# Row maxima of attention: transposed by VectorE and laid out through DRAM, with p x v groups cut at the ends of query blocks

## The chip, the cores and the metric

The kernel runs on one core of a Trainium2 chip. A core has five engines with queues of their own: TensorE (PE in the profile; PEld are its weight loads), VectorE (DVE), ScalarE (ACT), GpSimd (POOL) and SyncE (SP), which here only issues DMAs. The metric is device time in microseconds (us) of one execution.

## The reference

Two layers, each attention and then an MLP with Mish, both with a residual and a layer norm, over 2048 rows of 512 in float32. 32 heads of width 16:

```
scores = einsum("bhqd,bhkd->bhqk", q, k) * Dh ** -0.5
p = softmax(scores, axis=-1)
o = einsum("bhqk,bhkd->bhqd", p, v)
```

`x = x + A(norm(x)); x = x + B(norm(x))`, twice with the same weights. The softmax needs, for each query and head, the maximum of its row of scores before the first exp of that row.

## The kernel before

**Blocks and steps.** In attention the heads are taken in 8 groups of 4 (`NG`, `HG`), the queries in 4 blocks of 512 columns (`NCH`, `CW`). A block (one group, 512 queries; 32 per layer) has 16 steps, one per tile of 128 keys, with 4 heads in each; 512 steps per layer.

**The scores are computed twice.** First for the maxima (*M*, `max_mm`, L273): queries as stationary operand, 128 queries by 512 keys, two heads side by side in two halves of TensorE's rows (L293); VectorE reduces the 128x1024 scores from PSUM to two columns of maxima (L297). The PSUM tiles of M (`pm`) have two buffers. 32 M's make a block. Then for the exp (*P* and *S*): keys as stationary operand, 512 queries as columns, so that p stands with keys on the partitions as p x v needs it. *P* (`pair`, L338) computes two heads (L347) into two banks, of which there is one set (tag `s2`), and ScalarE takes the exp of both (L348). *S* (`single`, L350) does a third head (L357, L358) in one bank (tag `s1`).

**How the maximum gets into the exp.** The matmuls of P and S have 48 rows of split q and k, and two more, rows 48 and 49 of each half: ones on k's side (L249) and, on q's side, minus the maximum of each query in two parts, rounded and remainder. So the score comes out of TensorE with its maximum subtracted. For this the maxima, which lie with queries on the partitions (128x16: 4 heads by 4 tiles of 128 queries), must come to lie along a row. When the last M of a block has been reduced, `max_fold` (L306) reduces the four partial maxima (L308, 128x64 to 128x16). Four ticks later (a tick comes with every v, L422) `max_rows` (L311) transposes them on TensorE into the bank `s1` (L316), ScalarE copies them negated (L319), GpSimd makes the two parts (L320, L321) on 16x128, and SP issues eight DMAs of 2 KB from there into q's rows (L325).

**p x v** (*v*, `pv`, L360) accumulates over the keys of a block in one PSUM bank (`acc`): 4 heads in four column quarters, `va` with 32 columns per head as the stationary operand. Its work is counted in units of a quarter (128 query columns, all four heads); a step has 4 units and a block 64. Each v calls `pv(3 * done)`, so it does what is missing up to three units per v so far. At the end of a block it stops (`full`) until the bank has been drained: ScalarE copies it (L392), SP stores it (L393). The drain is called behind the next P, the following v takes up what was left.

**The order** is written out by hand, three steps at a time:

```
CYCLE = ("PMvSM", "PvMSPMv", "SMPvMS")
```

That is 4 P, 4 S, 6 M and 4 v per cycle of three steps, 12 units of p x v. `pe` chains TensorE's instructions in just this order; the other engines' queues are ordered by the framework's scheduler, except those calls that `behind` keeps in program order. M runs ahead by 24 steps (`AHEAD`), so a block's maxima are complete eight steps before its first P. SP's queue also carries the loads of q and k of the next group (`prep_qk`, two rows of ones among them), of v, and of weights; GpSimd's carries the splitting of weights (L132, L133) in the first layer.

Of the kernel before, what the change touches and what calls it, by code (L numbers as in the profile page):

```python
# [9 lines left out]
F32 = mybir.dt.float32  # L10
F32R = mybir.dt.float32r
BF16 = mybir.dt.bfloat16
AF = mybir.ActivationFunctionType
ALU = mybir.AluOpType
AX = mybir.AxisListType
# [3 lines left out]
P = 128  # L19
S, D, H, DH, F = 2048, 512, 32, 16, 1792  # L20
NCH = 4
CW = S // NCH
# [3 lines left out]
HG = 4  # L26
# [6 lines left out]
KROWS = 48  # L33
MROWS = 50
HALF = 64
K_PARTS = (0, 0, 1)
Q_PARTS = (0, 1, 0)
CYCLE = ("PMvSM", "PvMSPMv", "SMPvMS")
QW = CW // 4
AHEAD = 24  # L40
PRE = 4
FILL = 12
# [5 lines left out]
MAX_M = (6, 3, 7)  # L48
T_BUFS = {"he": 1, "hr": 1}
NBLK = 22  # L50


@with_exitstack
def kernel(ctx: ExitStack, tc: tile.TileContext, x, wqkv, wo, w1, b1, w2, out):
    nc = tc.nc
# [3 lines left out]
    const = ctx.enter_context(tc.tile_pool(name="const", bufs=1))  # L59
    blk = ctx.enter_context(tc.tile_pool(name="blk", bufs=NBLK))  # L60
    tmp = ctx.enter_context(tc.tile_pool(name="tmp", bufs=2))
    ps = ctx.enter_context(tc.tile_pool(name="ps", bufs=2, space=PSUM))
    dram = ctx.enter_context(tc.tile_pool(name="dram", bufs=1, space=DRAM))

    nc.scalar.preload_act_table_set("natural_log_exp_and_others")
    ident = const.tile([P, P], F32, name="ident")
# [2 lines left out]
    nc.gpsimd.memset(mhalf, -0.5)  # L69
    lnhalf = const.tile([P, 1], F32, name="lnhalf")  # L70
    nc.gpsimd.memset(lnhalf, LN_HALF)
    ones = const.tile([MROWS - KROWS, P], F32, name="ones")
    nc.gpsimd.memset(ones, 1.0)
    b1t = const.tile([P, FT], F32, name="b1t")
    nc.sync.dma_start(b1t, b1.rearrange("(f p) -> p f", p=P))

    def b8(shape, dt, name):
        return blk.tile(shape, dt, tag="blk", name=name)
# [3 lines left out]
    def open_banks():  # L82
        banks["pool"] = tc.tile_pool(name="sp", bufs=1, space=PSUM, reuse_waits="tile")
        banks["s"] = banks["pool"].__enter__()

    def close_banks():
        banks.pop("pool").__exit__(None, None, None)
        del banks["s"]
# [3 lines left out]
    def pbank(tag, name):  # L92
        if tag == "s":
            return banks["s"].tile([P, 512], F32, tag=tag, name=name, bufs=3)
        return ps.tile([P, 512], F32, tag=tag, name=name, bufs=1)
# [4 lines left out]
    def behind(ins):  # L100
        return tc.keep_in_program_order(ins)
# [110 lines left out]
    class Attention:  # L212
        def __init__(self, l, scr):
            self.l, self.scr = l, scr
            self.vscr = dram.tile([NG, P, NKT, HG * VW], F32, name=f"vscr{l}")
            self.oscr = [dram.tile([KT, 2, P, CW], F32, name=f"oscr{l}{c}") for c in range(NCH)]
            self.va = {}
            self.qk, self.mxs, self.pts, self.accs = {}, {}, [], {}
            self.singles, self.full, self.unit = 0, None, 0
            self.later = []  # L220
            self.chained, self.running, self.last = False, False, None

        def tick(self, n=1):
            due, self.later = [f for t, f in self.later if t <= n], [(t - n, f) for t, f in self.later if t > n]
            for f in due:
                f()

        def pe(self, ins):
            if self.chained:
# [9 lines left out]
        def prep_qk(self, g):  # L239
            l = self.l  # L240
            ks, qs = [], []
            for u in range(HG // 2):
                k = b8([P, S], F32R, f"ks{l}{g}{u}")
                q = b8([P, S], F32R, f"qs{l}{g}{u}")
                m, h0 = divmod(g * HG + 2 * u, P // DH)
                for e in range(2):
                    r0 = e * HALF
                    queue = nc.gpsimd if g == 0 and e else nc.sync
                    queue.dma_start(  # L249
                        k[r0 + KROWS : r0 + MROWS].bitcast(F32).rearrange("p (r n) -> p r n", n=P),  # L250
                        ones[:, None, :].to_broadcast([MROWS - KROWS, S // P, P]),
                    )
                    yield
                    for t, parts, base in ((k, K_PARTS, NCH), (q, Q_PARTS, 0)):
                        for j, a in enumerate(parts):
                            queue.dma_start(
                                t[r0 + j * DH : r0 + (j + 1) * DH].bitcast(F32),
                                self.scr[base + m][a, (h0 + e) * DH : (h0 + e + 1) * DH, :].bitcast(F32),
                            )
                            yield  # L260
                ks.append(k)
                qs.append(q)
            self.qk[g] = (ks, qs)
# [34 lines left out]
            if u == 1 and i == GSTEPS // 4 - 1:  # L298
                self.max_fold(b)

        def bank(self, name):
            if self.running:
                return self.pool.tile([P, CW], F32, tag="s1", name=name)
            return pbank("s", name)

        def max_fold(self, b):  # L306
            nm = tmp.tile([P, HG * NCH], F32, tag="nm", name=f"nm{self.l}{b}")
            nc.vector.tensor_reduce(nm, self.mxs.pop(b).rearrange("p h t a -> p (h t) a"), axis=AX.X, op=ALU.max)  # L308
            self.later.append((4, lambda: self.max_rows(b, nm)))

        def max_rows(self, b, nm):  # L311
            g, qb = divmod(b, NCH)
            l = self.l
            _, qs = self.qk[g]
            tp = self.bank(f"nmt{l}{b}")
            self.pe(nc.tensor.transpose(tp[0 : HG * NCH, 0:P], nm, ident))  # L316
            nf = tmp.tile([HG * NCH, P], F32, tag="nf", name=f"nf{l}{b}", bufs=1)
            np_ = tmp.tile([HG * NCH, 2, P], F32R, tag="np", name=f"np{l}{b}", bufs=1)
            nc.scalar.activation(nf, tp[0 : HG * NCH, 0:P], AF.Copy, scale=-1.0)  # L319
            behind(nc.gpsimd.tensor_copy(np_[:, 0], nf))  # L320
            behind(nc.gpsimd.tensor_tensor(np_[:, 1], nf, np_[:, 0].bitcast(F32), op=ALU.subtract))  # L321
            for h in range(HG):
                for a in range(2):
                    r = (h % 2) * HALF + KROWS + a
                    nc.sync.dma_start(  # L325
                        qs[h // 2][r : r + 1, ts(qb, CW)].bitcast(F32).rearrange("o (t n) -> o t n", n=P),
                        np_[h * NCH : (h + 1) * NCH, a, :].bitcast(F32),
                    )

        def head_rows(self, i):  # L330
            s, h = divmod(i, HG)
# [28 lines left out]
        def pv(self, upto):  # L360
            while self.unit < min(upto, 4 * STEPS):
# [3 lines left out]
                if kt == 0 and q0 == 0:  # L365
                    if self.full is not None:
                        return
                    self.accs[b] = pbank("acc", f"pv{self.l}{b}")
                cols = slice(q0 * QW, q1 * QW)
                for h in range(HG):  # L370
# [23 lines left out]

        def run(self, hooks, pre, fill):
            self.prep_v(0, range(NCH - 1))
            self.running = True
            left = 2 * PRE
            close_banks()
            with tc.tile_pool(name="sa", bufs=1, space=PSUM, reuse_waits="tile") as self.pool:  # L400
                half, done = 2 * (AHEAD + PRE), -4
                for s in range(STEPS + 4):
                    if s % GSTEPS == GSTEPS - NKT and s // GSTEPS + 1 < NG:
                        self.prep_v(s // GSTEPS + 1)
                    for item in CYCLE[s % 3]:
                        if item == "P":
                            self.pair()
                            self.drain()
                        elif item == "S":
                            self.single()  # L410
                        elif item == "M" and left:
                            left -= 1
                            next(pre)
                            next(pre)
                            if not left:
                                next(pre, None)
                                self.prep_v(0, [NCH - 1])
                        elif item == "M":
                            self.max_mm(half // 2, half % 2)
                            half += 1  # L420
                        else:
                            self.tick()  # L422
                            done += 1
                            self.pv(3 * done)
                    if s + FILL >= STEPS:
                        next(fill, None)
                    for fn in hooks.get(s, []):
                        fn()
                self.drain()
                self.tick(99)  # L430
            open_banks()

    def load_qkv(l, wts, which, later):
# [12 lines left out]
    def qkv(l, wts, tt, order, late, due):  # L446
        scr = [dram.tile([2, P, S], F32R, name=f"scr{l}{m}") for m in range(2 * NCH)]
        att = Attention(l, scr)
        ahead = [0]

        def some_max():
            if ahead[0] < AHEAD + PRE:
                att.tick()
                for n in range(2):
                    att.max_mm(ahead[0], n)
                ahead[0] += 1

        done = 0
# [33 lines left out]
        i = 0  # L492
# [185 lines left out]
    for l in range(2):  # L678
        due = {}
# [9 lines left out]
        att = qkv(l, wts, tt, order, late, due)  # L689
# [30 lines left out]
        for c, (t0, t1, t2, t3) in enumerate(((-42, -20, -19, -13), (-26, -19, -18, -11), (-10, -6, -4, 0))):  # L720
            o = outs[c]
# [89 lines left out]
```

## Time and profile before

| | |
|---|---|
| median of 3 runs | 3623.95 us (3623.9 to 3626.84) |
| the profiled execution | 3625.2 us; span of its instructions 3623.4 us |
| granted TensorE clock, mean | 0.997 of full speed |
| first P of the two layers | 186.2 and 1987.6 us |
| last drain of the two layers | 1460.1 and 3262.0 us |
| shares of the span | PE 98%, PEld 54%, DVE 82%, ACT 70%, POOL 16% |
| transposes of maxima (L316) | 64, 277 ns each |

Attention is thus some 1274 us of each layer; the rest is the projections, the MLP, and the norms. In a row of the groups' view stand line, engine, operation, output and inputs, shapes and count; then busy us, mean ns of one, and the engine's idle time before them with what ended it. In a row of the line of time stand start and length in us, both of equal instructions merged (x count), and in brackets the idle time before. The view of stretches gives length and busy us of each engine between two times.

### The profile page before, as it was taken

Reading aid. Unit: us, or ns where it says so; the run is one execution under the profiler, and the core shown is the slowest. Engines: PE = TensorE matmul, PEld = TensorE weight load, DVE = VectorE, ACT = ScalarE, POOL = GpSimd, SP = SyncE. Lnnn points to the kernel's source line nnn. Section 1 sums busy time; section 2 is a strip of 40 time slices with the busy share of each in tenths; the row PEclk is TensorE's granted clock in tenths of the full one; section 3 lists DMA queues with packets and bytes.
Section 4 is the critical chain, followed back from the end, with each engine's and each line's share of the span. In section 5 each row is a group of like instructions: output and inputs, shape, how many; then the busy total and the mean of one; then the engine's idle time right before and its main releaser. Section 6 shows DMA issues by size and latency. Waiting matters only on the chain. (4 is left out here: it accounts for less than half of the span.)

```text
span 3623.4 us, 69472 instructions
## 1 busy us (share of the span) xinstructions
PE 3553.0 (98%) x28784; PEld 1948.5 (54%) x28784; DVE 2963.7 (82%) x2978; ACT 2520.7 (70%) x3475; POOL 567.6 (16%) x589
## 2 busy tenths in 40 slices
PE   7999999999999999999999999999999999999999
PEld 5644444444444444777776444444444444447887
DVE  4779999999999994666647799999999999946565
ACT  2178888888888888344421788888888888873444
POOL 2200101001000002345421000000000000024455
PEclk9999999999999999999999999999999999999999
DMA  6551313313122224600164311112021211245000
GB/s 192 202 157 38 79 49 69 68 40 78 48 51 60 51 78 65 183 35 12 47 197 150 66 31 35 36 40 43 19 46 28 46 33 33 78 69 179 36 12 24
DMA packets 128707, 254.07 MB, mean 70 GB/s; under 512 B 18680, under 2 KB 62584, under 8 KB 114568
## 3 DMA queue, kind: packets, MB, share of 16 engines
q1 hardware_dynamic: 101896, 174.58, 19.8%
q0 software_dynamic: 8224, 35.21, 3.5%
q10 hardware_dynamic: 18272, 39.85, 3.0%
q8 instruction: 226, 3.70, 0.4%
q14 instruction: 89, 0.73, 0.1%
HBM read 148.38 MB, written 99.09 MB: 68 GB/s over the span
## 5 line engine op out<-in xcount | busy, mean ns | idle before, releaser
L297 DVE TENSOR_REDUCE mxv<-pm 128x2 f32<-128x1024 f32 x2048 | 2388.0, 1219 | 180.7 <-PE pm L293 132.7
L348 ACT ACTIVATE p<-sp 128x1024 f32<-128x1024 f32 x1366 | 1396.9, 1023 | 17.5 <-PE sp L347 12.3
L373 PE MATMUL pv<-p,va 128*32 128x128 f32 (+3 forms) x16048 | 1166.9, 392 | 0.0
L293 PE MATMUL pm<-ks,qs 48*128 48x512 f32 x4096 | 1106.8, 445 | 0.2
L358 ACT ACTIVATE p<-ss 128x512 f32<-128x512 f32 x1364 | 815.2, 598 | 384.7 <-PE ss L357 290.3
L347 PE MATMUL sp<-qs,ks 50*128 50x512 f32 x2732 | 737.8, 447 | 4.5 <-ACT p L348 2.2
L293 PEld LDWEIGHTS pm<-ks,qs 48*128 48x128 f32 x4096 | 460.0, 184 | 360.6 <-issue 256.8
L373 PEld LDWEIGHTS pv<-p,va 128*32 128x32 f32 x16048 | 368.2, 108 | 498.2 <-issue 417.8
L357 PE MATMUL ss<-qs,ks 50*128 50x512 f32 x1364 | 610.7, 448 | 0.1
L357 PEld LDWEIGHTS ss<-qs,ks 50*128 50x128 f32 x1364 | 252.0, 185 | 305.3 <-ACT p L358 210.6
L347 PEld LDWEIGHTS sp<-qs,ks 50*128 50x128 f32 x2732 | 276.7, 183 | 202.3 <-ACT p L348 117.3
L320 POOL CAST np<-nf 16x128 fp32r<-16x128 f32 x64 | 17.9, 280 | 2230.5 <-ACT nf L319 2188.2
L608 POOL TENSOR_TENSOR hb<-hb,he 128x512 f32<-128x512 f32 x112 | 157.6, 1407 | 188.2 <-DVE he L605 184.1
L611 POOL TENSOR_TENSOR hb<-hb,hr 128x512 f32<-128x512 f32 x112 | 160.4, 1432 | 137.3 <-DVE ah L610 129.5
L612 DVE TENSOR_TENSOR al<-hb,ah 128x512 fp32r<-128x512 f32 x112 | 108.0, 964 | 84.5 <-POOL hb L611 82.2
L606 ACT ACTIVATE hr<-he 128x512 f32<-128x512 f32 x112 | 70.8, 632 | 151.6 <-POOL hb L611 77.0
L154 ACT ACTIVATE pt<-qk 128x512 fp32r<-128x512 f32 x64 | 37.9, 598 | 158.9 <-PE qk L162 127.5
L604 ACT ACTIVATE he<-he 128x512 f32<-128x512 f32 x112 | 70.8, 632 | 102.9 <-DVE he L603 99.7
L602 ACT ACTIVATE hb<-h,b1t 128x512 f32<-128x512 f32 x112 | 76.8, 685 | 77.2 <-DVE al L612 52.0
L610 DVE TENSOR_TENSOR ah<-hb,hr 128x512 fp32r<-128x512 f32 x112 | 76.9, 687 | 61.4 <-ACT hr L607 34.3
L605 DVE SCALAR_TENSOR_TENSOR he<-he 128x512 f32<-128x512 f32 x112 | 79.9, 714 | 41.9 <-ACT he L604 39.1
L603 DVE TENSOR_SCALAR he<-hb 128x512 f32<-128x512 f32 x112 | 68.0, 608 | 48.5 <-POOL hb L608 33.9
(225 smaller groups left out, 3277.7 us busy)
## 6 DMA issues: line engine op xcount, KB each, us to landing
scr<-pt ACTq DMA_DIRECT2D x64, 512.0 KB
qs<-scr SPq DMA_DIRECT2D x180, 128.0 KB
ks<-scr SPq DMA_DIRECT2D x180, 128.0 KB
vscr<-v SPq DMA_DIRECT2D x32, 512.0 KB
va<-vscr SPq DMA_DIRECT2D x64, 256.0 KB
oscr<-ot SPq DMA_DIRECT2D x64, 256.0 KB
ww<-sw POOLq DMA_DIRECT2D x14, 1024.0 KB, 5.2
qs<-np SPq DMA_DIRECT2D x512, 2.0 KB
```

Source lines behind the costliest of these rows:

```text
L293: nc.tensor.matmul(pm[:, e], qs[u][rows, q0 : q0 + P], ks[u][rows, ts(n, 512)], start=True, stop=True)
L297: nc.vector.tensor_reduce(self.mxs[b][:, 2 * u : 2 * u + 2, qt, n], pm, axis=AX.X, op=ALU.max)
L347: self.pe(nc.tensor.matmul(sp[:, e], k, q, start=True, stop=True))
L348: nc.scalar.activation(self.pts[-1][:, 0:n], sp[:, 0:n], AF.Exp, scale=SCALE)
L357: self.pe(nc.tensor.matmul(sp, k, q, start=True, stop=True))
L358: nc.scalar.activation(self.pts[i // 3][:, 2], sp, AF.Exp, scale=SCALE)
L373: nc.tensor.matmul(self.accs[b][ts(h, VW), cols], self.va[b // NCH][:, kt, h, :], self.pts[j][:, e, cols], start=kt == 0 and q0 == 0, stop ...
L605: nc.vector.scalar_tensor_tensor(e, e, 2.0, e, op0=ALU.add, op1=ALU.mult)
L608: nc.gpsimd.tensor_tensor(hb, hb, e, op=ALU.mult)
L610: nc.vector.tensor_tensor(ah, hb, r, op=ALU.mult)
L611: nc.gpsimd.tensor_tensor(hb, hb, r, op=ALU.mult)
L612: nc.vector.tensor_tensor(al, hb, ah.bitcast(F32), op=ALU.subtract)
```

## The change

Two parts. **The maxima** no longer pass through TensorE, PSUM and ScalarE. The fold writes 16 of the 32 columns of a tile whose others are zero (two such tiles, in turn); VectorE transposes each 32x32 block of it (128x32), so that in every quarter of 32 partitions 16 rows hold the maxima of 32 queries. GpSimd makes the two parts from that, now on 128x32 and in two buffers. SP writes them to DRAM in four DMAs, one per quarter, and reads them back in four, one per head, each with both of q's rows. The sign moves from ScalarE's copy to k's rows, which become minus ones. `tick` and its delay go: all of it follows the fold at once. **The groups of p x v**: `pv(3 * done)` becomes `pv(units(done))`; over 64 v's, 192 units and three blocks, a v does three units except for the 21st and 42nd, which do four, and the 63rd and 64th, which do two. So the 21st, 42nd and 64th end a block.

```diff
+def units(done):
+    n, i = divmod(max(done, 0), 64)
+    if i < 22:
+        u = 3 * i + (i == 21)
+    elif i < 43:
+        u = 64 + 3 * (i - 21) + (i == 42)
+    else:
+        u = 128 + 3 * (i - 42) - (i == 63)
+    return 192 * n + u
...
-    ones = const.tile([MROWS - KROWS, P], F32, name="ones")
-    nc.gpsimd.memset(ones, 1.0)
+    minus = const.tile([MROWS - KROWS, P], F32, name="minus")
+    nc.gpsimd.memset(minus, -1.0)
+    folded = [const.tile([P, TR], F32, name=f"folded{i}") for i in range(2)]
+    for t in folded:
+        nc.gpsimd.memset(t, 0.0)
...
         def max_fold(self, b):
-            nm = tmp.tile([P, HG * NCH], F32, tag="nm", name=f"nm{self.l}{b}")
-            nc.vector.tensor_reduce(nm, self.mxs.pop(b).rearrange("p h t a -> p (h t) a"), axis=AX.X, op=ALU.max)
-            self.later.append((4, lambda: self.max_rows(b, nm)))
-
-        def max_rows(self, b, nm):
             g, qb = divmod(b, NCH)
             l = self.l
             _, qs = self.qk[g]
-            tp = self.bank(f"nmt{l}{b}")
-            self.pe(nc.tensor.transpose(tp[0 : HG * NCH, 0:P], nm, ident))
-            nf = tmp.tile([HG * NCH, P], F32, tag="nf", name=f"nf{l}{b}", bufs=1)
-            np_ = tmp.tile([HG * NCH, 2, P], F32R, tag="np", name=f"np{l}{b}", bufs=1)
-            nc.scalar.activation(nf, tp[0 : HG * NCH, 0:P], AF.Copy, scale=-1.0)
-            behind(nc.gpsimd.tensor_copy(np_[:, 0], nf))
-            behind(nc.gpsimd.tensor_tensor(np_[:, 1], nf, np_[:, 0].bitcast(F32), op=ALU.subtract))
+            nm = folded[b % 2]
+            nc.vector.tensor_reduce(
+                nm[:, 0 : HG * NCH], self.mxs.pop(b).rearrange("p h t a -> p (h t) a"), axis=AX.X, op=ALU.max
+            )
+            nt = tmp.tile([P, TR], F32, tag="nt", name=f"nt{l}{b}")
+            nc.vector.transpose(nt, nm)
+            np_ = tmp.tile([P, 2, TR], F32R, tag="np", name=f"np{l}{b}")
+            behind(nc.gpsimd.tensor_copy(np_[:, 0], nt))
+            behind(nc.gpsimd.tensor_tensor(np_[:, 1], nt, np_[:, 0].bitcast(F32), op=ALU.subtract))
+            nd = dram.tile([HG * NCH, 2, P // TR, TR], F32, name=f"nd{l}{b}")
+            for j in range(P // TR):
+                nc.sync.dma_start(nd[:, :, j], np_[j * TR : j * TR + HG * NCH].bitcast(F32))
             for h in range(HG):
-                for a in range(2):
-                    r = (h % 2) * HALF + KROWS + a
-                    nc.sync.dma_start(
-                        qs[h // 2][r : r + 1, ts(qb, CW)].bitcast(F32).rearrange("o (t n) -> o t n", n=P),
-                        np_[h * NCH : (h + 1) * NCH, a, :].bitcast(F32),
-                    )
+                r = (h % 2) * HALF + KROWS
+                nc.sync.dma_start(
+                    qs[h // 2][r : r + 2, ts(qb, CW)].bitcast(F32).rearrange("a (t n) -> a t n", t=NCH),
+                    nd[ts(h, NCH)].rearrange("t a j r -> a t (j r)"),
+                )
...
-                            self.tick()
                             done += 1
-                            self.pv(3 * done)
+                            self.pv(units(done))
```

In the built program TensorE has 64 transposes and 8 matmuls of p x v fewer (8016 for 8024, as the program writes them), ScalarE 64 copies fewer, VectorE 64 transposes more; GpSimd's and SP's counts stay, but for two memsets. The order of all other instructions on TensorE, VectorE and GpSimd is the same; on ScalarE the drain moves with the block's end.

More of the change, by code (lines that the diff above doesn't have):

```diff
@@ L39 @@
 QW = CW // 4
+TR = 32
 AHEAD = 24
@@ L219, in __init__ @@
             self.singles, self.full, self.unit = 0, None, 0
[L220 to L226, printed above, removed]
+            self.chained, self.last = False, None
         def pe(self, ins):
@@ L250, in prep_qk @@
                         k[r0 + KROWS : r0 + MROWS].bitcast(F32).rearrange("p (r n) -> p r n", n=P),
-                        ones[:, None, :].to_broadcast([MROWS - KROWS, S // P, P]),
+                        minus[:, None, :].to_broadcast([MROWS - KROWS, S // P, P]),
                     )
@@ L299, in max_mm @@
                 self.max_fold(b)
[L301 to L304, printed above, removed]
         def max_fold(self, b):
-            nm = tmp.tile([P, HG * NCH], F32, tag="nm", name=f"nm{self.l}{b}")
-            nc.vector.tensor_reduce(nm, self.mxs.pop(b).rearrange("p h t a -> p (h t) a"), axis=AX.X, op=ALU.max)
-            self.later.append((4, lambda: self.max_rows(b, nm)))
-        def max_rows(self, b, nm):
             g, qb = divmod(b, NCH)
@@ L396, in run @@
             self.prep_v(0, range(NCH - 1))
-            self.running = True
             left = 2 * PRE
@@ L429, in run @@
                 self.drain()
-                self.tick(99)
             open_banks()
@@ L452, in some_max @@
             if ahead[0] < AHEAD + PRE:
-                att.tick()
                 for n in range(2):
```

## The prediction

> **What bounds the kernel now.** I read the page first (busy shares), then TensorE's line of time in the attention phase, then sums over stretches, and last the waits around the transpose of the maxima.
>
> ```profile
> PE 3553.0 (98%) x28784; PEld 1948.5 (54%) x28784; DVE 2963.7 (82%) x2978; ACT 2520.7 (70%) x3475; POOL 567.6 (16%) x589
> ```
>
> TensorE is busy almost all the time, but its ends are modelled, so a share alone proves little. The view that decides is that of stretches. In attention the same work recurs every three steps (4 P, 4 S, 6 M, 4 v). I cut at the p x v matmul with which this cycle begins, and lay beside each other quiet cycles, cycles with a transpose of the maxima, and cycles in which a block of queries ends. Columns: length, then busy us of PE, PEld, DVE, ACT and POOL.
>
> ```profile
> core 0: us, PE busy (x) PEld busy (x) DVE busy (x) ACT busy (x) POOL busy (x), PEclk, DMA share, GB/s
> 403.69:410.90 7.21, 7.21 (x75) 3.28 (x73) 6.99 (x7) 6.14 (x9) 0.00 (x0) 1.00 0.98 130
> 410.90:418.66 7.76, 7.53 (x76) 3.39 (x74) 7.31 (x9) 6.25 (x10) 0.73 (x2) 1.00 0.14 19
> 447.55:455.27 7.72, 7.51 (x75) 3.42 (x74) 7.57 (x9) 6.62 (x10) 0.00 (x0) 1.00 0.01 2
> 491.78:499.46 7.68, 7.46 (x75) 3.46 (x74) 7.09 (x8) 6.26 (x10) 0.73 (x2) 1.00 0.00 1
> 475.27:482.88 7.61, 7.46 (x66) 3.06 (x64) 6.99 (x7) 6.52 (x10) 0.00 (x0) 1.00 0.09 34
> 513.87:521.28 7.41, 7.41 (x66) 3.09 (x64) 6.96 (x7) 6.46 (x10) 0.00 (x0) 1.00 0.40 94
> 399.24:516.83 117.59, 116.77 (x1142) 52.82 (x1139) 112.07 (x100) 99.65 (x135) 10.18 (x12) 1.00 0.22 58
> ```
>
> A quiet cycle takes 7.2 us, PE busy throughout, at full clock. The last row holds three blocks, from one drain to the third after it: 16 cycles, which at 7.2 would be 115.2. So 117.59 - 115.2 = 2.39 us per three blocks are not the steady state. Rows two to four hold one transpose each and are 0.55, 0.51 and 0.47 us over the quiet 7.21: 1.53 together. The other 0.86 belongs to block ends: 0.40 in row five, 0.20 in row six, the rest in small pieces.
>
> VectorE is close behind:
>
> ```profile
> 402.58 9.54 DVE L297 TENSOR_REDUCE mxv<-pm 128x2 f32<-128x1024 f32 x8
> 412.15 0.22 DVE L308 TENSOR_REDUCE nm<-mxv 128x16 f32<-128x64 f32 x1
> 412.29 5.89 DVE L297 TENSOR_REDUCE mxv<-pm 128x2 f32<-128x1024 f32 x5
> 451.40 4.61 DVE L297 TENSOR_REDUCE mxv<-pm 128x2 f32<-128x1024 f32 x4
> L308 DVE TENSOR_REDUCE nm<-mxv 128x16 f32<-128x64 f32 x64 | 13.9, 217 | 1.5
> PEld pm L293 <- DVE mxv L297: 86.1, 181, 0.6
> PEld pm L293 <- DVE nm L308: 12.5, 20, 0.6
> ```
>
> A reduce lasts 1.22 us, but four in a row take 4.61: they start (4.61 - 1.22) / 3 = 1.13 us apart. Six are 6.78 of the 7.2 us, so VectorE has about 0.4 us to spare per cycle, 2.2 us per block of 5.33 cycles, of which the fold (L308, 217 ns) takes 0.25. It is a near second. The two waits show that already: 181 loads of M's weights waited for a reduce, 20 for the fold.
>
> **The change, part by part.**
>
> *The transpose leaves TensorE.* What it costs is not its 277 ns:
>
> ```profile
> 415.74 0.51 PE L347 MATMUL sp<-qs,ks 50*128 50x512 f32 x2
> 416.08 0.40 PE L293 MATMUL pm<-ks,qs 48*128 48x512 f32 x2
> 416.71 0.28 PE L316 MATMUL nmt<-ident,nm 128*16 128x128 f32 x1 [0.23 <-ACT p L358]
> 416.92 0.85 PE L373 MATMUL pv<-p,va 128*32 128x384 f32 x8
> 416.06 0.60 ACT L358 ACTIVATE p<-ss 128x512 f32<-128x512 f32 x1 [0.37 <-PE ss L357]
> ```
>
> M's matmuls end at 416.08 + 0.40 = 416.48; the transpose starts 0.23 us later, and p x v 0.21 us after that. The transpose takes the single bank of the S scores, and waits until ScalarE's exp (416.06 + 0.60 = 416.66) has emptied it. With the matmul go the wait and ScalarE's copy (L319). What is late next? The p x v behind it needs only an old p; the next S finds the bank free, as in every quiet cycle. So I take the whole excess: 1.53 us per three blocks. There are 64 folds, 62 of them inside the two attention phases (31 each; each layer's first is transposed while q, k and v are made): 62 / 3 x 1.53 = **31.6 us off**. Below: VectorE keeps part of it, priced next. Above: no more than this.
>
> *The transpose goes to VectorE.* The trace shows no transpose there. The nearest row by size is the fold, 217 ns for 64 elements a partition; the transpose moves 32. On the built program's order the transpose stands one reduce behind the fold in two blocks of three, and right behind it in the third. With a reduce between, it overlaps as reduces do (1.22 - 1.13 = 0.09) and takes 217 - 90 = 0.13 us; right behind, it waits for the fold as the fold waits for its reduce and takes about 0.25 us. What queues behind it are reduces, and behind those M's on TensorE, by two PSUM buffers. Bounds: below, nothing (the 0.4 us of slack per cycle hides it, as the fold is hidden in most blocks); above, all of it on the path, 62 x 0.25 = 15.5 us. I take 0.05 us per block, since only 20 of 64 folds were waited for: **3.1 us on**.
>
> [...]
>
> *The groups of p x v.* Before, each v does up to 3 units; a block is 64, so two ends of three fall inside a group:
>
> ```profile
> 476.48 0.53 PE L347 MATMUL sp<-qs,ks 50*128 50x512 f32 x2
> 476.94 0.43 PE L373 MATMUL pv<-p,va 128*32 128x128 f32 x8
> 478.19 0.50 PE L347 MATMUL sp<-qs,ks 50*128 50x512 f32 x2
> 478.85 1.28 PE L373 MATMUL pv<-p,va 128*32 128x512 f32 x16
> 477.11 1.02 ACT L348 ACTIVATE p<-sp 128x1024 f32<-128x1024 f32 x1
> 515.78 0.64 PE L373 MATMUL pv<-p,va 128*32 128x256 f32 x8
> ```
>
> At 476.94 only one unit is done; TensorE runs ahead by about 0.4 us, and the next P (478.19) stands until the exp of the P before it (477.11 + 1.02 = 478.13) frees its banks. The two units that are missing follow as a group of five (478.85), so what was stalled is lost: the 0.40 of row five. At 515.78 the group has two units, one short: row six, 0.20. After the change a block end is reached with groups of 4, 4 and, before the third end, 2 and 2. A long group stalls nothing, as ScalarE (6.14 of 7.21) and VectorE then catch up. The two short ones, each one unit short, cost 0.20 apiece by row six. So 0.40 + 0.20 becomes 0.20 + 0.20; the remaining 0.26 stays. Gain 0.20 per three blocks: 62 / 3 x 0.20 = **4.1 us off**. Bounds: nothing, and all 0.86 (17.8 us). The count of groups stays, so no matmul time is saved.
>
> *The way through DRAM.* GpSimd's two operations work on 128x32 instead of 16x128, a quarter of the elements per partition (280 and 450 ns now, taken as the upper end); the splits of weights that share its queue leave it idle for 107 of the 117.59 us. SP's eight DMAs per block stay eight: four writes, then four reads that wait for them. It costs nothing if the rows arrive before the block's first P:
>
> ```profile
> 491.78 0.21 DVE L308 TENSOR_REDUCE nm<-mxv 128x16 f32<-128x64 f32 x1
> 509.78 0.56 PE L347 MATMUL sp<-qs,ks 50*128 50x512 f32 x2
> 418.08 5.05 SPq L325 DMA_DIRECT2D qs<-np  x8
> L320 POOL CAST np<-nf 16x128 fp32r<-16x128 f32 x64 | 17.9, 280 | 2230.5 <-ACT nf L319 2188.2
> L321 POOL TENSOR_TENSOR np<-nf,np 16x128 fp32r<-16x128 f32 x64 | 28.8, 450 | 5.1
> 1460.71 0.34 SPq L393 DMA_DIRECT2D oscr<-ot  x1
> 1462.86 1.71 SPq L539 DMA_DIRECT2D den<-oscr  x4
> rec<-rscr POOLq DMA_DIRECT2D x64, 128.0 KB, 5.6
> ```
>
> From the end of that fold (491.99) to the block's first P there are 17.8 us, in the tightest of the three patterns. Needed: a reduce between and the transpose 1.35, GpSimd 0.73, four issues 2.5 (half of 5.05), a landing, four issues 2.5, a landing. A write to DRAM that a read on SP waits for took 1460.71 to 1462.86 = 2.15 us, issue included. With 2.15 twice the chain is 11.4 us, 6.4 to spare; the four steps that the transpose was held back before (412.37 to 416.71, 4.3 us) are saved, and SP's other loads move by the 2 us that SP now stands. **Nothing.** What is behind SP then are loads for the next group and the drains' stores, which SP awaits for most of a block anyway.
>
> **The sum.** The profiled execution took 3625.2 us (span 3623.4 and 1.8 around it): 3625.2 - 31.6 + 3.1 - 4.1 = 3592.6. It stands 1.25 above the median of the runs, 3623.95, so I expect a median of **3591**.
>
> **The rivals.**
>
> *VectorE keeps more* (0.14). Every transpose is exposed in full and the group change brings nothing: 3623.95 - 31.6 + 15.5 = 3608. For it speaks the 0.4 us of slack; against it that the fold, longer or as long, was waited for in 20 blocks of 64.
>
> *Block ends become free too* (0.08): 3623.95 - 31.6 - 17.8 = 3574.5. Against it speak the two short groups.
>
> *The bank wait only moves* (0.05). If the S scores' bank is what paces TensorE, the next S takes over the wait, and the time stays at 3624. Against it: quiet cycles use the same bank in the same order and show no idle PE.
>
> *VectorE, not TensorE, is the bound* (0.06, slower). Then the 1.53 us were VectorE's in any case, and each transpose is added: 62 x 0.13 to 62 x 0.25, or 8 to 15 us, 3632 to 3639. It decides once six reduces, fold and transpose exceed the cycle for good: 6.78 + 0.25 + 0.25 = 7.28 against 7.21, true in the one cycle that has all three, not over a block (36.7 of 38.4 us). Against it also: a cycle with a transpose on TensorE grows by its full 0.5 us, which a bound on VectorE would have swallowed.
> [...]
>
> *The rows come late* (0.03, slower). With a landing of 5.6 us each, the row of the loads on GpSimd's queue, the chain is 18.3 us and the first P of each block waits 0.5 us; beyond 5.35 us a landing this decides.
>
> **How the numbers follow.** The forecast has 0.64. Faster by over 0.2% (about what a measurement of this kernel tells from no change, 7 us): 0.64 + 0.14 + 0.08 = 0.86; within 0.2%: 0.05; slower: 0.09. The range takes in the bounds of VectorE's price and of the block ends, 3574 to 3610, and leaves out 0.14.
>
> **What would show it.** Right: cycles with a fold at 7.2 to 7.3 us, three blocks in about 115.8 to 116.2, no PE idle before p x v there. Wrong: M's that wait for the transpose in most blocks (VectorE), idle PE before a block's first P that a DMA ends (rows late), or stalls at S of 0.3 us as before (the bank). A transpose of 0.5 us or more on VectorE would undo the sum.

## The result and the profile after

| | before | after |
|---|---|---|
| median (5 runs each) | 3623.9 us (3616.7 to 3626.84) | 3586.16 us (3581.18 to 3589.2) |
| the profiled execution | 3625.2 us | 3589.2 us |
| its span | 3623.4 us | 3587.4 us |
| granted TensorE clock, mean | 0.997 | 0.997 |

The ratio is 0.9903, with a 95% interval of 0.9891 to 0.9914. The change makes the kernel some 1% faster; the two profiled executions lie 36.0 us apart. The executions of two experiments below (three hops, one late block) lie far apart, and are given one by one.

The busy shares of the changed kernel, from its page:

```profile
PE 3540.3 (99%) x28704; PEld 1942.6 (54%) x28704; DVE 2967.9 (83%) x3042; ACT 2518.1 (70%) x3411; POOL 550.4 (15%) x591
```

TensorE is busy for 12.7 us less, and the span is 36.0 us shorter. That takes in the phases outside attention. In attention idle time of PE is somewhat less than half of the gain: three blocks lost 0.82 us of it (PE was busy for 116.77 of 117.59 us, now for all of 115.80) and 0.97 us of busy time. The view of stretches shows where. I cut the cycles at the first P of every four, a few tenths of a us away from the cuts of the prediction. A quiet cycle comes first, then three with a transpose of the maxima on VectorE, then the three ends of blocks (four units, four units, two and two), and last sixteen cycles, three blocks.

```profile
core 0: us, PE busy (x) PEld busy (x) DVE busy (x) ACT busy (x) POOL busy (x), PEclk, DMA share, GB/s
398.80:406.01 7.21, 7.21 (x76) 3.27 (x74) 6.98 (x6) 6.13 (x8) 0.00 (x0) 1.00 0.51 85
406.01:413.24 7.23, 7.23 (x75) 3.35 (x72) 7.01 (x8) 6.16 (x8) 0.45 (x2) 1.00 0.02 3
449.34:456.56 7.22, 7.22 (x75) 3.36 (x73) 7.16 (x8) 6.14 (x8) 0.45 (x2) 1.00 0.04 9
485.59:492.79 7.20, 7.20 (x76) 3.31 (x74) 7.10 (x8) 6.12 (x8) 0.46 (x2) 1.00 0.02 3
470.96:478.40 7.44, 7.44 (x76) 3.32 (x74) 7.07 (x6) 6.56 (x9) 0.00 (x0) 1.00 0.09 35
507.18:514.60 7.42, 7.42 (x68) 3.15 (x65) 6.98 (x6) 6.66 (x9) 0.00 (x0) 1.00 0.16 41
427.73:434.90 7.17, 7.17 (x69) 3.07 (x66) 6.97 (x7) 6.22 (x9) 4.00 (x3) 1.00 0.14 56
398.80:514.60 115.80, 115.80 (x1140) 52.46 (x1137) 112.24 (x102) 99.62 (x131) 9.35 (x12) 1.00 0.20 53
```

Before, a cycle with a transpose took 7.68 to 7.76 us; now these three take 7.20 to 7.23, a quiet cycle's 7.21. (Averaged over all blocks, the three patterns take 7.29, 7.23 and 7.20.) Three blocks took 117.59 us, now 115.80, and PE has no idle time in them. What is left over 16 x 7.2 = 115.2 stands at the ends of blocks. The line of time of TensorE shows their groups: four units, and the two groups of two.

```profile
471.63 1.07 PE L377 MATMUL pv<-p,va 128*32 128x512 f32 x8
432.01 0.64 PE L377 MATMUL pv<-p,va 128*32 128x256 f32 x8
433.65 0.64 PE L377 MATMUL pv<-p,va 128*32 128x256 f32 x8
```

A group of three lasts 0.85 us, so a unit of p x v is 0.21 to 0.22 us. The cycle with four units does one unit more and is 0.22 us longer: it stalls nothing. The cycle with two and two does two units less, 0.43 us of work, and is still only 0.04 shorter: each short group loses 0.2 us there.

Averaged over all cycles of both attention phases (cycles 16 to 144 of each), three blocks took 117.61 us before and 115.85 after, 1.76 less. With 62 / 3 = 20.67 such threes this is 36.4 us, which accounts for the whole difference of the two profiles (36.0). This mean length of three blocks is used below: it leaves out the phases that the change doesn't touch.

On VectorE fold, reduce and transpose stand as follows in the line of time (two blocks of the three patterns):

```profile
409.62 0.22 DVE L316 TENSOR_REDUCE folded<-mxv 128x16 f32<-128x64 f32 x1
409.94 0.21 DVE L320 STREAM_TRANSPOSE nt<-folded 128x32 f32<-128x32 f32 x1
410.08 28.28 DVE L307 TENSOR_REDUCE mxv<-pm 128x2 f32<-128x1024 f32 x24
448.17 0.22 DVE L316 TENSOR_REDUCE folded<-mxv 128x16 f32<-128x64 f32 x1
448.31 1.22 DVE L307 TENSOR_REDUCE mxv<-pm 128x2 f32<-128x1024 f32 x1
449.44 0.20 DVE L320 STREAM_TRANSPOSE nt<-folded 128x32 f32<-128x32 f32 x1
449.56 25.06 DVE L307 TENSOR_REDUCE mxv<-pm 128x2 f32<-128x1024 f32 x21
```

The groups by shape give mean ns of one behind the busy time; the waits give us in total, times, and the longest:

```profile
L320 DVE STREAM_TRANSPOSE nt<-folded 128x32 f32<-128x32 f32 x64 | 13.1, 205 | 2.4
L322 POOL CAST np<-nt 128x32 fp32r<-128x32 f32 x64 | 13.3, 208 | 2214.2 <-DVE nt L320 2214.2
L323 POOL TENSOR_TENSOR np<-nt,np 128x32 fp32r<-128x32 f32 x64 | 16.0, 251 | 5.1
```

```profile
PEld pm L303 <- DVE mxv L307: 105.3, 216, 0.8
PEld pm L303 <- DVE folded L316: 25.0, 40, 0.6
```

The transpose lasts 205 ns. Behind a reduce the next instruction starts 0.12 us after it (449.44 to 449.56); right behind the fold, 0.46 us pass from the fold's start to that of the next reduce. GpSimd's two operations fell from 280 and 450 to 208 and 251 ns. M's loads of weights wait somewhat more often for VectorE than before (216 and 40 times, for 181 and 20), but these are waits of the weight loads, which overlap with matmuls here (in the last row of the stretches they are busy for 52.46 of 115.80 us, and the matmuls for all of it).

### The profile page after: what moved, and what is told of

It is laid out like the page before. It is cut to its first block, busy times and chain, and to the rows that moved or that the text cites. A ratio compares the mean times of both kernels' runs of the same rounds, so it can differ in the third digit from the quotient of the medians.

```text
span 3587.4 us, 69160 instructions
## 1 busy us (share of the span) xinstructions
PE 3540.3 (99%) x28704; PEld 1942.6 (54%) x28704; DVE 2967.9 (83%) x3042; ACT 2518.1 (70%) x3411; POOL 550.4 (15%) x591
## 4 chain that ended last, share of the span: by engine, by line
PE 49%; DVE 1%; DMA 1%; ACT 1%; issue 0%; POOL 0%; POOLq 0%; DVEq 0%; ACTq 0%; SPq 0%
PE pv L377 15%; PE pm L303 9%; PE ss L361 6%; PE sp L351 5%; PE mo L178 2%; PE h L176 2%; PE h L178 2%; PE h L177 2%; PE mo L176 2%; PE mo L177 2%; PE qk L176 1%; PE qk L178 1%; PE qk L177 1%; PE va L176 0%; DMA ks<-scr 0%
## 5 line engine op out<-in xcount | busy, mean ns | idle before, releaser
L377 PE MATMUL pv<-p,va 128*32 128x256 f32 (+2 forms) x16032 | 1167.0, 392 | 0.1
L351 PE MATMUL sp<-qs,ks 50*128 50x512 f32 x2732 | 726.5, 447 | 0.3
L303 PEld LDWEIGHTS pm<-ks,qs 48*128 48x128 f32 x4096 | 450.6, 184 | 345.1 <-issue 210.8
L351 PEld LDWEIGHTS sp<-qs,ks 50*128 50x128 f32 x2732 | 261.8, 183 | 200.8 <-ACT p L352 119.5
L322 POOL CAST np<-nt 128x32 fp32r<-128x32 f32 x64 | 13.3, 208 | 2214.2 <-DVE nt L320 2214.2
```

The lines of the kernel that those rows point to most:

```text
L303: nc.tensor.matmul(pm[:, e], qs[u][rows, q0 : q0 + P], ks[u][rows, ts(n, 512)], start=True, stop=True)
L351: self.pe(nc.tensor.matmul(sp[:, e], k, q, start=True, stop=True))
L377: nc.tensor.matmul(self.accs[b][ts(h, VW), cols], self.va[b // NCH][:, kt, h, :], self.pts[j][:, e, cols], start=kt == 0 and q0 == 0, stop ...
```

## The experiments

Two theories stood against each other for the larger part of the gain. *The bank*: the transpose on TensorE was dear because it had to wait for the bank of S, and a transpose that waits for nothing would cost little. *The rival*: the matmul itself, between others, costs most of it. For VectorE the rivals were that its transpose is exposed, or that VectorE is the bound. The edits are against the changed kernel, where not said otherwise.

**The two parts by themselves.** First the maxima alone:

```diff
-                            self.pv(units(done))
+                            self.pv(3 * done)
```

> The maxima's new way alone, p x v groups as before. Theory (the transpose's excess on TensorE goes, VectorE gives 3.1 us back): 3624 - 31.6 + 3.1 = 3595 us; cycles that had a transpose fall to 7.2 to 7.3 us, block ends keep their 0.40 and 0.20. Rival (the gain is the block ends'): 3615 or more.

Measured: 3594.38 us, ratio 0.9928 (0.9916 to 0.9941). Three blocks take 116.08, 1.52 less than before.

Then the groups alone, an edit of the kernel before (with `units` as in the change):

```diff
-                            self.pv(3 * done)
+                            self.pv(units(done))
```

> The new groups of p x v alone, transposes on TensorE as before. Theory: two short groups cost 0.20 each in place of 0.40 and 0.20, so 3624 - 4 = 3620 us. Rival (block ends become free): 3606 us.

Measured: 3615.41 us, ratio 0.9985 (0.9976 to 0.9994). Three blocks take 117.37, 0.24 less. The parts add up: 1.52 + 0.24 = 1.76, the change as a whole. By these, the maxima are worth 1.52 x 20.67 = 31.4 us and the groups 0.24 x 20.67 = 5.0.

**What the transpose costs VectorE.** Once none, and once three for one:

```diff
-            nt = tmp.tile([P, TR], F32, tag="nt", name=f"nt{l}{b}")
-            nc.vector.transpose(nt, nm)
+            nt = nm
```

> The changed kernel without VectorE's transposes: GpSimd reads the folded maxima untransposed, so the rows subtracted are not the queries' maxima. Theory (VectorE's slack hides most of a transpose): 3 us under the changed kernel, about 3583. Rival (VectorE keeps all of it): 8 to 15 us under it, 3571 to 3578.

Measured: 3585.12 us, ratio 0.9898 (0.9884 to 0.9911); three blocks 115.81, 0.03 less than with the transpose. Single cycles don't show the price: one pattern of fold falls from 7.29 to 7.21, another rises from 7.23 to 7.31.

```diff
+            for _ in range(2):
+                spare = tmp.tile([P, TR], F32, tag="nx", name=f"nx{l}{b}{_}")
+                nc.vector.transpose(spare, nm)
             nc.vector.transpose(nt, nm)
```

> The changed kernel with two more transposes of the same tile by VectorE per block, their results unused. Theory (slack of 0.4 us per cycle, mostly enough for one, not for three): 5 to 15 us more, 3591 to 3601. Rival (VectorE hides them all): 3586. Rival (VectorE is the bound): their whole length, 62 x 2 x 0.2 = 25 us more, 3611.

Measured: 3589.84 us, ratio 0.9915 (0.9902 to 0.9929); three blocks 115.95, 0.10 more. Six transposes add 0.10 us, 0.016 each, and the first three 0.01 each. Transposes in a row overlap: from the start of the first to that of the next reduce, three of them take 0.32 us on average, one takes 0.13. So the six are some 0.6 us of VectorE's time, and its slack hides most of it. That is below what I had expected. By the cycles, the change's transposes together cost 0.03 x 20.67 = 0.6 us, 1 us at most; the medians are too coarse to tell it from nothing.

**Is VectorE the bound?** Its reduces are made short, over half of the scores:

```diff
-            nc.vector.tensor_reduce(..., pm, axis=AX.X, op=ALU.max)
+            nc.vector.tensor_reduce(..., pm[:, :, 0:256], axis=AX.X, op=ALU.max)
```

> The changed kernel with M's reduce over 256 of each 512 columns: maxima of half the keys, VectorE's work in attention about halved. Theory (TensorE is the bound): quiet cycles stay at 7.2 us, and only the waits of M for VectorE go, 3578 to 3584. Rival (VectorE is the bound): cycles fall well under 7.0 us and the time by over 60 us.

Measured: 3583.47 us, ratio 0.9896 (0.9881 to 0.9911). The group of the reduces, and the same sixteen cycles in the view of stretches:

```profile
L307 DVE TENSOR_REDUCE mxv<-pm 128x2 f32<-128x512 f32 x2048 | 1415.0, 693 | 1085.7 <-PE pm L303 1019.9 <-PE ss L361 58.9 <-PE sp L351 0.8
```

```profile
398.80:514.60 115.80, 115.80 (x1148) 52.28 (x1140) 67.86 (x103) 99.75 (x132) 9.38 (x12) 1.00 0.22 58
```

VectorE is busy for 67.86 instead of 112.24 us, and the stretch still takes 115.80. Over all cycles three blocks take 115.66, 0.19 less, some 4 us in the kernel. So TensorE sets the pace, and VectorE, 97% busy in the changed kernel (112.24 of 115.80), was not the bound.

**Short groups.** Groups of 4 and 2 units in turn instead of threes:

```diff
-    if i < 22:
-        u = 3 * i + (i == 21)
-    elif i < 43:
-        u = 64 + 3 * (i - 21) + (i == 42)
-    else:
-        u = 128 + 3 * (i - 42) - (i == 63)
-    return 192 * n + u
+    j = i if i < 21 else i - 21 if i < 42 else i - 42
+    u = 64 * min(i // 21, 2) + 3 * j + j % 2
+    return 192 * n + u - 2 * (i == 63)
```

> The changed kernel with groups of p x v of four and two units in turn (4, 2, 4, 2, ...), blocks ending at the same v's: 32 short groups per three blocks instead of 2. Theory (a short group sends the next P into the exp before it, 0.2 us each, and nothing gives it back): 30 x 0.2 x 62 / 3 = 124 us more, about 3710. Rival (what costs at a block's end is the drain of its bank): no change, 3586.

Measured: 3694.2 us, ratio 1.0204 (1.019 to 1.0218). Three blocks take 121.24, 5.39 more. With 30 more short groups in them that is 0.18 us for each, close to the 0.20 of the prediction. The amount of work is the same, and still it takes longer: what a short group leaves undone is not made up by the long one.

**Is the wait for the bank the cost?** An edit of the kernel before: the transpose is put behind p x v instead of ahead of it, so that exp has emptied the bank by then.

```diff
-                            self.tick()
                             done += 1
                             self.pv(3 * done)
+                            self.tick()
```

> The kernel before with the transpose called behind the v instead of ahead of it, when ScalarE has long emptied the bank of the S scores. Theory (half of the 0.5 us is the wait for that bank): the transpose starts at once, but the S that follows waits for ScalarE's copy; some 0.2 to 0.3 us per block less, 3605 to 3612. Rival (it is the matmul and its switch that cost): 3624.

Measured: 3621.99 us, ratio 1.0005 (0.9996 to 1.0014). This missed: nothing was gained. The line of time, and behind it the waits (us in total, times, longest), show why.

```profile
409.80 0.85 PE L373 MATMUL pv<-p,va 128*32 128x384 f32 x8
410.59 0.28 PE L316 MATMUL nmt<-ident,nm 128*16 128x128 f32 x1
411.22 0.50 PE L357 MATMUL ss<-qs,ks 50*128 50x512 f32 x1 [0.35 <-ACT nf L319]
```

```profile
PEld ss L357 <- ACT nf L319: 25.2, 62, 0.9
PE ss L357 <- ACT nf L319: 9.3, 22, 0.7
```

The transpose now follows p x v at once, as wanted. But the next S needs the same bank, and its weight load waits for ScalarE's copy of the maxima (`nf`) after all 62 transposes. In 22 blocks S is the next instruction, and PE itself stands, 9.3 / 22 = 0.42 us; such a cycle is 0.7 us longer than a quiet one. There the wait has only moved, from the exp ahead of the transpose to the copy behind it. In the other 40 an M lies between, and PE has no idle time around the transpose; the cycles are still some 0.46 us longer. The transpose's own time is part of that, and S starts later beside its M (0.43 to 0.49 us behind it, for 0.34 in a quiet cycle); I did not take the rest apart. What the transpose costs without any bank to wait for, this run can't say. That is the next one: a transpose on TensorE, 62 times, into the bank that the next M writes anyway, with nothing that reads it.

```diff
+            if b and u == 0 and i == 6:
+                self.pe(nc.tensor.transpose(pm[0 : HG * NCH, 0, 0:P], folded[(b - 1) % 2][:, 0 : HG * NCH], ident))
```

> The changed kernel with the same transpose on TensorE once more, 62 of them, just ahead of an M and into that M's own PSUM tile, which the M then overwrites: the matmul without the bank of the S scores and without ScalarE's copy; its result is unused. Theory (of the 0.5 us per block 0.2 is TensorE's own time and 0.3 the bank's chain): 62 x 0.2 = 13 us over the changed kernel, 3599. Rival (all of it is the matmul and its switch): 32 us over it, 3618.

Measured: 3606.56 us, ratio 0.9962 (0.9948 to 0.9976), about 21 us over the changed kernel; three blocks take 116.84, 1.0 more. Read as a sum this would make 0.33 us of each transpose TensorE's own, more than I had given to it. But the three transposes of three blocks cost 0.21, 0.41 and 0.42 us (mean cycles of 7.50, 7.61 and 7.65 against 7.29, 7.20 and 7.23), by what stands around them. Two of the places in the line of time:

```profile
413.84 0.85 PE L379 MATMUL pv<-p,va 128*32 128x384 f32 x8
414.63 0.28 PE L301 MATMUL pm<-ident,folded 128*16 128x128 f32 x1
414.83 0.50 PE L305 MATMUL pm<-ks,qs 48*128 48x512 f32 x2
...
452.73 0.50 PE L363 MATMUL ss<-qs,ks 50*128 50x512 f32 x1
453.15 0.28 PE L301 MATMUL pm<-ident,folded 128*16 128x128 f32 x1
453.36 0.50 PE L305 MATMUL pm<-ks,qs 48*128 48x512 f32 x2
```

Behind p x v the transpose takes 414.83 - 414.63 = 0.20 us. Between S and M (and between P and M, the third place) it is dearer. S and M use half of the rows each and run side by side: M normally starts 0.01 us behind such an S (273.40 and 273.41 in the changed kernel, shown further below). Here the transpose begins 0.42 us after S, and M 0.21 us after it: what would run side by side runs one by one. The transpose itself uses all 128 rows (128x16 stationary).

In the kernel before, none of the 62 transposes stood in such a place: p x v always came right behind them. So its own share there is the 0.21 us, and the rest can be read from the kernel before itself, in its waits:

```profile
PE nmt L316 <- ACT p L358: 13.4, 62, 0.2
```

All 62 transposes waited for the exp, 13.4 / 62 = 0.22 us each. Of the 1.52 / 3 = 0.51 us that one of them cost, 0.22 are idle time ahead of it, 0.21 its own, and 0.08 I didn't take apart; most of that, by my estimate, is that p x v starts some 0.07 us before the matmul ahead of it has ended, where nothing is waited for (in a quiet cycle of the kernel before at 405.62 us, behind an M that ends at 405.27 + 0.42).

**When the rows come late.** DMAs from DRAM to DRAM are put between writing and reading: three per block, six per block, and seven for one block alone (block 5 of the first layer).

```diff
+            for x in range(3):
+                nx = dram.tile([HG * NCH, 2, P // TR, TR], F32, name=f"nx{l}{b}{x}")
+                nc.sync.dma_start(nx, nd)
+                nd = nx
```

> The changed kernel with the maxima copied three more times from DRAM to DRAM before they are read back. From the fold to the last issue of the read-back 6.8 us pass, of 17.9 to the block's first P; a copy is about 2.2 us. Theory (11 us to spare): no change, 3586. Rival (the rows are close to late): some us per block, 3650 or more.

Measured: 3846.4, 4456.77, 3662.81 and 3752.74 us, median 3799.57. This missed by far. I had gone by a typical block of the changed kernel: 17.9 us from the fold's end to the block's first P, and the last read issued 6.8 us after the fold. (The median to the first scores that need the rows is 17.4 us: every third block begins with an S, ahead of its first P.) The tightest block, the third of the first layer, has much less. In the changed kernel's line of time:

```profile
256.32 0.21 DVE L316 TENSOR_REDUCE folded<-mxv 128x16 f32<-128x64 f32 x1
257.57 0.20 DVE L320 STREAM_TRANSPOSE nt<-folded 128x32 f32<-128x32 f32 x1
257.84 0.21 POOL L322 CAST np<-nt 128x32 fp32r<-128x32 f32 x1 [17.73 <-DVE nt L320]
258.01 2.38 POOL L149 TENSOR_TENSOR swo<-rwo,swo 128x1024 fp32r<-128x1024 f32 x1
260.35 0.25 POOL L323 TENSOR_TENSOR np<-nt,np 128x32 fp32r<-128x32 f32 x1
260.62 3.26 SPq L326 DMA_DIRECT2D nd<-np  x4
264.73 1.20 SPq L144 DMA_DIRECT2D rw<-in_B_w_dram  x1
266.80 1.14 SPq L329 DMA_DIRECT2D qs<-nd  x4
273.40 0.50 PE L361 MATMUL ss<-qs,ks 50*128 50x512 f32 x1
273.41 0.72 PE L303 MATMUL pm<-ks,qs 48*128 48x512 f32 x2
```

A splitting of weights (L149, 2.38 us) stands between GpSimd's two operations and other loads between SP's write and read. The last read is issued 266.80 + 1.14 - 256.53 = 11.4 us after the fold, and the block's first scores, the S at 273.40 us, come 5.5 us later. Three hops take about 6.8 us (261.54 to 268.33 us on SP in the experiment). So in the experiment the rows of that block come late, by little, and what follows is not little. TensorE's line of time (that block's first S, and another wait of the same execution, which is taken up at the end), and then the stretches ahead of the first wait, behind it, and later:

```profile
269.79 0.47 PE L365 MATMUL ss<-qs,ks 50*128 50x512 f32 x1 [1.55 <-DMA qs<-nx]
3429.07 0.69 PE L355 MATMUL sp<-qs,ks 50*128 50x512 f32 x1 [1.69 <-DMA qs<-nx]
```

```profile
200.00:268.00 68.00, 68.00 (x682) 31.17 (x681) 64.44 (x60) 57.82 (x77) 4.84 (x7) 1.00 0.47 97
272.00:620.00 348.00, 348.00 (x1914) 148.74 (x1913) 200.44 (x172) 172.25 (x222) 14.15 (x19) 0.50 0.13 35
630.00:1340.00 710.00, 709.05 (x6958) 322.42 (x6954) 687.20 (x627) 608.58 (x802) 55.47 (x73) 1.00 0.24 61
```

TensorE waits for 1.55 us, and then has a granted clock of 0.50 for 351.6 us (271.9 to 623.4), though it is busy all the time. Matmuls come at 5.5 per us there, for 10.0 ahead of it. A wait of 2.7 us, at 1354.7 us, comes with another 218.5 us at half clock. In all, TensorE waited for rows in five blocks, 8.2 us together.

> The same with six copies, about 13 us more than the changed kernel where some 9 to 11 are to spare. Theory (the way through DRAM is free only as long as it is shorter than the lead of M): 2 to 4 us per block, 3710 to 3830. Rival (SP's queue or the rows are not what P waits for): 3586.

Measured: 5363.26 us (5314.39 to 5381.39), ratio 1.479 (1.4729 to 1.4852), at a mean clock of 0.632 in the profiled execution. This missed too, by 1500 us and more. The loss is far larger than the waits, ten for rows with 30.1 us in all; most of attention runs at half clock:

```profile
860.00:2190.00 1330.00, 1330.00 (x7310) 568.23 (x7308) 764.71 (x657) 657.23 (x844) 44.24 (x65) 0.50 0.13 36
3000.00:4880.00 1880.00, 1880.00 (x10350) 802.82 (x10354) 1076.92 (x927) 929.75 (x1195) 16.26 (x63) 0.50 0.10 24
```

In both runs several blocks wait. The last run has a single late block, so that one wait stands alone; seven hops for it:

```diff
+            for x in range(7 if (l, b) == (0, 5) else 0):
```

> The changed kernel with seven extra copies from DRAM to DRAM for one block only, the sixth of the first layer: its rows come some 3 to 6 us after TensorE first wants them. Theory (a late row costs its wait and then a long stretch at half the granted clock, as in the runs with three and six copies for every block): one wait, then the clock at 0.5 for 85 us or more, 40 to 160 us over the changed kernel, 3626 to 3746. Rival (a wait costs its length, and the clock is back after some us, as elsewhere in this kernel): 3 to 10 us, 3589 to 3596.

Measured: 3747.05, 4364.95, 3659.74 and 3691.0 us, median 3719.03. The profiled execution (3747.05 us):

```profile
392.12 0.76 PE L365 MATMUL ss<-qs,ks 50*128 50x512 f32 x1 [8.09 <-DMA qs<-nx]
```

```profile
395.00:745.00 350.00, 350.00 (x1923) 149.74 (x1919) 201.43 (x173) 172.78 (x223) 14.15 (x19) 0.50 0.15 35
750.00:1340.00 590.00, 590.00 (x5796) 268.19 (x5795) 571.68 (x520) 506.41 (x668) 42.69 (x57) 1.00 0.23 59
```

One wait of 8.09 us; half clock from 388.6 us on, for 358.4 us. At 5.49 matmuls per us for 9.82, that costs 358.4 x (1 - 5.49 / 9.82) = 158 us, and with the wait 166; measured are 161 over the changed kernel's median. The four executions put the price of the same single wait at 74, 105, 161 and 779 us, and their mean granted clocks fall with it: 0.977, 0.967, 0.951 and 0.796. The long half clock came as expected; the size, 40 to 160 us, did not cover it.

## Why the prediction was right, point by point

**The forecast.** 3591 us, measured 3586.16. Of the 4.8 us between them, 2.9 are the maxima (28.5 net forecast, 31.4 by the cycles) and 0.9 the groups; the rest is within the interval.

**The bound.** TensorE sets the pace in attention: shown by halved reduces (0.19 us per three blocks). The reading of cycles against the quiet 7.2 us carried the sum.

**The transposes leave TensorE.** Predicted 31.6 us off, less 3.1 for VectorE, 28.5 net; measured 31.4 net in the trace of the maxima alone. By the medians of that run and of the kernel before beside it, 3620.96 - 3594.38 = 26.6, with an interval (0.9916 to 0.9941) of 21 to 30 us. The cycles' 31.4 lies a little above that interval; why, no run shows.

**Why they cost that.** Here the reason was right by half. The prediction put the cost on the wait for the bank and ScalarE's copy, "not its 277 ns". The wait is 0.22 us of 0.51 by the row of the waits; the matmul's own 0.21 weighs as much, and the rows of the prediction (416.71 to 416.92) had it in plain sight. So, by an estimate from the two prices measured, a transpose on TensorE that waits for nothing would still cost 62 x 0.21 = 13 us at the best place, and 62 x 0.42 = 26 at a bad one.

**The bank wait only moves** (a rival). For the change it did not: with the transpose gone nothing uses that bank but S. In the experiment that only moved the transpose, it did: the weights of the next S waited for the copy in all 62 blocks, and PE itself in 22. The price that the prediction gave that case, no gain, is what was measured there.

**VectorE's price.** Predicted 3.1 us (0.05 per block, between 0 and 0.25); measured 0.01 to 0.016 per block, 0.6 to 1.0 us. It is the mis-sized term of the sum. The durations were right (0.12 behind a reduce, predicted 0.13; 205 ns, predicted 217), but the slack of 0.4 us per cycle takes them in. The 20 folds that were waited for, the row by which I chose 0.05, cost nothing much either: these were waits of weight loads, and all that a much faster VectorE brought was 0.19 us per three blocks.

**VectorE is the bound** (a rival): refuted by the halved reduces (VectorE busy for 67.86 instead of 112.24 us of the same stretch, which still took 115.80).

**The groups.** Predicted 4.1 us, measured 5.0 in the trace and 5.5 (3620.96 - 3615.41) by the medians, of which the interval allows 2 to 9. The mechanism, a short group loses 0.20 and a long one stalls nothing, is shown by the groups of 4 and 2 (0.18 each) and by the ends' cycles above. What is left of it, two short groups per three blocks, some 0.4 us, is most of the 115.85 - 115.2 = 0.65 us that the cycles still have over the quiet ones.

**The way through DRAM.** Predicted nothing, and nothing waits for it in the changed kernel. The estimate of 11.4 us for the chain took in the last landing; measured up to the last read's issue, the tightest block needs 11.4 and the median one 6.8, and the four reads there take 1.14 us to issue, not 2.5. The 17.8 us of room were misread by 0.4: that block begins with an S, 17.4 us behind the fold. The pattern was the tightest one, but within it the block that matters is an early one, where a split of weights and other loads stand in the chain's way.

**The rows come late** (a rival). Its mechanism was sound, but the price was wrong in kind: the prediction charged the length of the wait (0.5 us per block). One wait, 8.09 us long in the profiled execution, cost 74 to 779 us, by a clock that stays at half (0.50 for 358.4 us there). The chance that the rival got was low for a good reason, 5.5 us of room in the tightest block, yet its loss would have exceeded the whole gain.

**Not settled.** Why the clock stays at half for hundreds of us while TensorE is busy all the time. The length of the wait doesn't decide it. In the run with three hops one of 1.55 us did it, and in the same execution one of 1.34 us (up to 1643.42 us) led to only 3.4 us at half clock, one of 1.69 us (up to 3429.07) to 6.8, and one of 0.95 us (up to 733.59) to none; with six hops one of 1.19 us (up to 2975.4) was followed by 1918 us. The two short stretches stand behind the last M of their layer (1623.3 and 3408.6 us), where TensorE has another mix of matmuls; whether that is the reason no run tests. The length of half clock differs between executions of one kernel (74 to 779 us of loss). No run tells what ends it. The last 0.08 us of a transpose's 0.51 were not measured by themselves.

## What to carry to other kernels

Cut a repeated schedule into its cycles and lay those with an extra instruction beside those without: the difference prices the instruction with all that hangs on it, and here the sum was right even where the reason was not. A small matmul that uses all rows, put between matmuls that use half of the rows each, cost twice its own time here (0.42 us for 0.21), since it parts what runs side by side (M started 0.63 us behind S instead of 0.01); VectorE, with some 0.4 us of slack per cycle, took it for 0.01 to 0.016 us. Give rows that TensorE waits for room by the tightest block, not the median one, because the price of one late arrival here is not its length (one wait of 8.09 us where it was profiled, 74 to 779 us of loss).

## What the hardware showed

**The clock after a wait.** The kernel before and the changed one run all attention at a granted clock of 1.00 (the view of stretches, from each layer's first P to its last drain). One wait of 1.55 us, in the run with three hops, was followed by 351.6 us at 0.50, and one of 8.09 us, up to 392.12, came with 358.4 us of it from 388.6 on, TensorE busy throughout (348.00 of 348.00 and 350.00 of 350.00 us in the rows above). With six hops per block the half clock lasts through stretches of 1330 and 1880 us.

**Half-row matmuls around one that uses all rows.** A transpose of 128x16 cost 0.21 us behind p x v and 0.41 to 0.42 between P or S and M, as shown above by the bare transposes.

**VectorE's overlap.** The transposes between reduces cost less than their length here: 205 ns each, 0.12 to 0.14 us from the start of one to that of the reduce behind it (449.44 to 449.56, 409.94 to 410.08), and 0.01 to 0.016 us of the kernel's time per transpose.
